# The second product of 512-row expert tiles, made as seven products of quarters behind the transforms

## The chip, the cores and the metric

The kernel runs on one core of one Trainium2 chip. The core has TensorE (PE; its weight loads are shown apart as PEld), VectorE (DVE), ScalarE (ACT), GpSimd (POOL) and SyncE (SP), which issue their instructions in order, each from its own queue. The metric is the time of one execution on the device in microseconds.

## The reference

The first block filters eight sequences of 2496 tokens with 256 features in the frequency domain; the second sends each of the 19968 filtered tokens through one of eight experts, the one with the largest logit.

```python
X = np.fft.rfft(x, axis=1)                       # x: (8, 2496, 256)
y = np.fft.irfft(X * (filt_r + 1j * filt_i), n=2496, axis=1)
x = y.reshape(19968, 256)
logits = x @ w_gate                              # 8 experts
e = argmax(logits); gate = softmax(logits)[e]
h = np.maximum(x @ w1[e], 0.0)                   # 256 -> 1024, for the rows of expert e
out = gate * (h @ w2[e])                         # 1024 -> 256
```

All operands are 32-bit floats. The two expert products are the bulk of the work.

## The kernel before, in words

**Transforms and routing.** The Fourier transforms are made as small matrix products in four stages (`stage_a` to `stage_d`), batch after batch. Behind each batch its tokens are routed: the logits are made, each token gets a row in a list of its expert, and POOL scatters the rows to a DRAM tensor, `rows`. After each batch a tile map (`tile_map`, line 839) takes full tiles out of the lists, so that expert tiles run beside the transforms of later batches.

**Expert tiles.** A tile is 512, 256 or 128 rows of one expert. `TILES` lists their sizes: 28 tiles of 512 rows in all, then 256-row tiles of the last batch (`PLACE` is the first of these) and 128-row tiles (`SHORT` is the first). For each tile SP loads the rows (`xg`, `ng`), DVE transposes them to `xT` (`turn_x`), and two streams of work on TensorE follow, in an order found while the program is built:

- The first product (`first_products`, `hidden_by_quarters`) makes h = relu(x·w1), one half of its 1024 columns after the other, into two buffers `hT` of a tile. For 512-row tiles, and for the 256-row tiles of the last batch, each half is made by seven products of quarters instead of eight: POOL first makes sums of quarters of x (`sums`, four operations) and of w1 (`wsum`, four operations per half, `w1_sums`), and DVE adds the products up. A half has 14 matmuls.
- The second product (`second_products`, `result`) makes 128 rows of the output at a time: eight matmuls of 128x128 weights (a piece of h) with 256 columns of w2, accumulated in one PSUM bank. DVE or ACT multiplies by the gate into `ys` (four buffers), and POOL scatters `ys` to the output with an indirect DMA. Each scatter to the output waits on the semaphore of the one before it, since both write the same tensor.

**Weights.** SP loads the two halves of a tile's w1 (`w1t`, three buffers) and w2 (`w2t`, two buffers) with `weights`, which `prefetch` calls when a buffer is free. Once the transforms are done (`late` is set), w2 of all experts is loaded piece by piece to stay (`w2s`), for the tiles from `PLACE` on, and the padding at the ends of the eight lists is scattered to `rows` by POOL (`pad_rows`, eight scatters), one with each call of `result` in the last batch.

**Order.** `Order` estimates when each engine is free and each tile is ready, and the loop at the end of the kernel picks the next transform step or expert product by these times. The order of instructions in each queue is fixed in this way when the program is built; on the chip, semaphores alone decide when each starts. The seven PSUM banks of the pool `ps` are given out in turn. All recorded operations show line 238, the one that issues them.

The lines that the steps below touch:

```python
w2t[h] = pools["moe"].tile([P, FH2, D], F32, tag="w2t", name="w2t", bufs=2)        # weights
h - used[what] < ((3 if h < 2 * SHORT else 8) if what == "w1" else 2 if h < 2 * PLACE else 8)   # prefetch
yield lambda: result(i, j), 3.42, ("w2", 2 * i + 1)                               # second_products
moe_w2=inputs["moe_w2"].reshape(E, 2, FT // 2, P, D).transpose(0, 1, 3, 2, 4),     # host
```

Of the kernel before, what the change touches and what calls it, by code (L numbers as in the profile page):

```python
# [19 lines left out]
P = 128  # L20
S = 2496
D = 256
E = 8
# [15 lines left out]
FT = F // P  # L39
# [227 lines left out]
def kernel(  # L267
# [55 lines left out]
    one = perm.tile([1, E], F32, name="one")  # L323
# [3 lines left out]
    ps = open_pool(ctx, name="ps", bufs=7, space=PSUM)  # L327
# [26 lines left out]
    vld = cst.tile([P, 2 * NG + 2], F32, name="vld")  # L354


    first = ExitStack()
    pro = open_pool(first, name="pro", bufs=2, side="right")
    tau_i = pro.tile([1, 32], I32, name="tau_i", bufs=1)
    e_i = pro.tile([P, E], I32, name="e_i", bufs=1)  # L360
    pools = {}
# [5 lines left out]
    def bank():  # L367
        return ps.tile([P, 512], F32, tag="bank", name="bank")


    t = nc.t
# [527 lines left out]
    FH2 = FT // 2  # L899
    TILES = [(rows // P, b) for b, g in enumerate(GROUPS) for rows, n in g for _ in range(n)]  # L900
    NT = len(TILES)
# [2 lines left out]
    SHORT = next(i for i in range(NT) if TILES[i][0] == 1)  # L904

    PLACE = next(i for i in range(NT) if TILES[i] == (2, B - 1))
    late = {}

    def quarters(i):
# [23 lines left out]
    def weights(h, second):  # L933

        i, k = divmod(h, 2)
        if late and second:

            for _ in range(1 if i < PLACE else 2 * E):
                if late["n"] < 2 * E:
                    e, hf = divmod(late["n"], 2)  # L940
                    nc.sync.dma_start(out=late["w2s"][:, e, hf * FH2:(hf + 1) * FH2], in_=moe_w2[e, hf])
                    late["n"] += 1
        if second and i >= PLACE:
            return
        ev = nc.sync.value_load(work[i][1], min_val=0, max_val=E - 1)
        if second:
            w2t[h] = pools["moe"].tile([P, FH2, D], F32, tag="w2t", name="w2t", bufs=2)
            nc.sync.dma_start(out=w2t[h], in_=moe_w2[bass.ds(ev, 1), k].rearrange("o p i d -> p (o i) d"))
        else:
            pool, bufs = (late["w1"], 8) if i >= SHORT else (pools["moe"], 3)  # L950
            w1t[h] = pool.tile([P, DH, 2, 2 * P], F32, tag="w1t", name="w1t", bufs=bufs)
            nc.sync.dma_start(out=w1t[h], in_=moe_w1[bass.ds(ev, 1), k].rearrange("o p i h f -> p (o i) h f"))
# [16 lines left out]
    def w1_sums(h):  # L969

        w = w1t[h]
        ts = wsum[h] = pools["moe"].tile([P, 3, 2 * P], F32, tag="wsum", name="wsum", bufs=2)
        nc.gpsimd.tensor_tensor(ts[:, 0], w[:, 0, 1], w[:, 1, 1], op=ALU.add)
        nc.gpsimd.tensor_tensor(ts[:, 1], ts[:, 0], w[:, 0, 0], op=ALU.subtract)

        nc.gpsimd.tensor_tensor(w[:, 0, 1], w[:, 0, 0], w[:, 0, 1], op=ALU.subtract)
        nc.gpsimd.tensor_tensor(ts[:, 2], w[:, 1, 0], ts[:, 1], op=ALU.subtract)
# [64 lines left out]
    def result(i, j):  # L1042
        n, e, r, b = work[i]
        if i >= PLACE:
            ev = nc.tensor.value_load(e, min_val=0, max_val=E - 1)
        if b == B - 1 and i < SHORT:
            next(late["pads"], None)
        p = bank()
        for k in range(FT):
            w2 = late["w2s"][:, bass.ds(ev, 1), k, :] if i >= PLACE else w2t[2 * i + k // FH2][:, k % FH2, :]  # L1050
            mm(p[:, :D], lhsT=hs[i][k % 4 // 2][:, k // 4, k % 2, j * P:(j + 1) * P], rhs=w2, start=(k == 0), stop=(k == FT - 1))
        ys = pools["moe"].tile([P, D], F32, tag="ys", name="ys", bufs=4)
        gate = gis[i][:, j, 8:9]
        either(p, D, lambda: nc.vector.tensor_scalar(ys, in0=p[:, :D], scalar1=gate, scalar2=None, op0=ALU.mult),
               lambda: nc.scalar.activation(ys, p[:, :D], AF.Copy, scale=gate))
        nc.gpsimd.indirect_dma_start(
            out=out,
            out_offset=bass.IndirectOffsetOnAxis(ap=gis[i].bitcast(U32)[:, j, :1], axis=0),
            in_=ys,
            in_offset=None,  # L1060
            bounds_check=N - 1,
            oob_is_err=False,
        )


    sides = []

# [62 lines left out]
    for k in range(B + 1):  # L1130
        steps = slot(k)
# [54 lines left out]
    def prefetch():  # L1186

        i = got["x"]
        if i < min(len(work), NT - RARE) and rows_at[work[i][3]] <= t["tensor"] and i - used["x"] < 2:
            rows_in(i)  # L1190
            asked.add(("x", i))
            got["x"] += 1
        for what in ("w1", "w2"):
            h = got[what]
            if h < 2 * min(len(work), NT - RARE) and rows_at[work[h // 2][3]] <= t["tensor"] and (
                    h - used[what] < ((3 if h < 2 * SHORT else 8) if what == "w1" else 2 if h < 2 * PLACE else 8)):
                weights(h, what == "w2")
                asked.add((what, h))
                got[what] += 1
        for h in range(used["w1"], got["w1"]):  # L1200
            if quarters(h // 2) and h not in wsum and len(wsum) < 2 and nc.ready(w1t[h]) <= max(t["tensor"], t["gpsimd"]) + 0.3:
                w1_sums(h)

    def when(key):

        what, n = key
        i = n // 2
        if what == "w2":
            if halves[0] <= n or key not in asked:
                return None  # L1210
            return max(ps.free("bank"), nc.ready(*hs[i], *((late["w2s"],) if i >= PLACE else (w2t[2 * i], w2t[2 * i + 1]))))
        if key not in asked or what != "x" and n % 2 and ends[0] < i:
            return None
        if what == "x":
            return nc.ready(xgs[n]) if t["vector"] < nc.ready(xgs[n]) else 0.0
        if what == "w1":
            return max(ps.free("bank"), nc.ready(w1t[n], xts[i]))
        return max(ps.free("bank"), ps.free("bank", 1) - 0.85, nc.ready(wsum[n], sums[i], xts[i]))
# [40 lines left out]
    def second_products():  # L1259

        for i in range(NT - RARE):
            for j in range(TILES[i][0]):
                yield lambda: result(i, j), 3.42, ("w2", 2 * i + 1)
            hs.pop(i), gis.pop(i), w2t.pop(2 * i, None), w2t.pop(2 * i + 1, None)
            used["w2"] += 2
            ends[0] += 1

    def rare_tiles():

# [17 lines left out]
    with tc.manual_schedule(engines=None):  # L1287
# [35 lines left out]
        while fs or any(heads):  # L1323
            choice = [(f, wait_of(f)) for f in open_steps()]
            products = []
            for k in (turn, 1 - turn):
                ready_at = when(heads[k][2]) if heads[k] else None
                if ready_at is not None:
                    products.append((k, max(0.0, ready_at - t["tensor"])))
            known = bool(products)  # L1330
            choice[0 if credit > 0.0 or not fs else 1:0] = products
            choice = [c for c in choice if c[1] is not None]
            pick, late_by = next((c for c in choice if c[1] <= 0.2), min(choice, key=lambda c: c[1]) if choice else (None, 0.5))
            if late_by > 0.2:
                t["tensor"] += min(late_by, 0.5)
            elif isinstance(pick, int):
                heads[pick][0]()
                credit -= heads[pick][1]
                if heads[pick][1] > 0.0:
                    turn = 1 - pick  # L1340
                heads[pick] = next(streams[pick], None)
            else:
                fs.remove(pick)
                pick[1]()
                credit = (credit if known else 0.0) + share() * pick[3]
                left_t[0] -= pick[3]
            flush()
            more_loads()
            for _ in range(4):
                side()  # L1350
            if not fs and not sides and not late:
                fft.close()
                tail = late["tail"] = open_pool(ctx, name="tail", bufs=1)
                late["w1"] = open_pool(ctx, name="w1b", bufs=8)
                late["n"] = 0
                late["pads"] = pad_rows()
                late["w2s"] = tail.tile([P, E, FT, D], F32, name="w2s")
            prefetch()
            if used["x"] > SHORT and "need" not in late:
                late["need"] = nc.values_load(need, min_val=0, max_val=GROUPS[-1][-1][1])  # L1360
# [32 lines left out]
```

## Time and profile before

| What | Value |
|---|---|
| time before, median of 3 runs | 1496.27 us (1493.14 to 1499.45) |
| the profiled execution's own time | 1494.36 us |
| its span, first to last instruction | 1492.7 us |
| TensorE busy | 1451.7 us (97%) |
| DVE, ACT, POOL busy | 770.7, 471.8, 733.4 us |
| granted TensorE clock | 0.991 |
| second product from `w2t` | 1984 records of 256 columns (992 matmuls) |
| DVE hT<-bank,hT of 512 elements | 392, mean 686 ns |
| POOL scatters to the output | 161, mean 998 ns |

All times of single instructions come from the one profiled execution, whose own time stands 1.9 us below the median. The 1.7 us between its span and its time lie around the program. In the profile a busy share of TensorE near 100% says that its queue never runs dry; a group's "idle before" names what ended the waiting of that engine, and only where TensorE is the one that waits does it lengthen the run by itself. In timelines the columns are start in us, length in us, engine, line, operation, output<-inputs, shapes and count, and in brackets the idle time before it with what ended it.

### The profile page before, as it was taken

How to read it: one execution, taken by the hardware profiler on the slowest of the kernel's cores; microseconds unless marked ns; L12 is line 12 of the kernel's file. 1: busy time of each engine (PE TensorE's matmuls, PEld its weight loads, DVE VectorE, ACT ScalarE, POOL GpSimd, SP SyncE). 2: the span in 40 equal slices, each digit the busy share in tenths (PEclk: the TensorE clock that was granted, in tenths of full speed). 3: DMA queues.
4: the chain of work that ended last, by engine and by line, in shares of the span. 5: the costliest groups of instructions: out<-in, count | busy, mean ns of one | idle time of the engine just before them, and what ended most of it. 6: DMA issues, size and time to landing. Idle time of an engine off the chain costs nothing. (4 is left out here: it accounts for less than half of the span.)

```text
span 1492.7 us, 24448 instructions
## 1 busy us (share of the span) xinstructions
PE 1451.7 (97%) x7396; PEld 1148.8 (77%) x7396; DVE 770.7 (52%) x1732; ACT 471.8 (32%) x983; POOL 733.4 (49%) x1053
## 2 busy tenths in 40 slices
PE   8898997999989999999999999999999999999998
PEld 6553555776667777777787888887888889999997
DVE  4667677354577656565764555537344334441110
ACT  4453442333322233222233222222222222223332
POOL 3434455344446656554555756764546455741111
PEclk9999999999999999999999999999999999999999
DMA  9749889678767756474456545545455543456661
GB/s 255 252 152 333 289 306 295 207 258 280 251 182 229 219 157 169 131 239 128 128 152 196 130 117 149 147 139 145 151 178 176 167 146 106 117 187 179 181 179 52
DMA packets 216376, 278.10 MB, mean 186 GB/s; under 512 B 124131, under 2 KB 163708, under 8 KB 216245
## 3 DMA queue, kind: packets, MB, share of 16 engines
q1 hardware_dynamic: 197125, 233.19, 52.7%
q0 software_dynamic: 19120, 43.33, 8.3%
q8 instruction: 62, 1.02, 0.3%
q14 instruction: 69, 0.57, 0.1%
HBM read 196.45 MB, written 80.64 MB: 186 GB/s over the span
## 5 line engine op out<-in xcount | busy, mean ns | idle before, releaser
L238 DVE TENSOR_TENSOR hT<-bank,hT 128x512 f32<-128x512 f32 (+1 forms) x504 | 300.7, 627 | 298.9 <-PE bank L238 183.1
L238 PE MATMUL bank<-w2t,hT 128*128 128x256 f32 x1984 | 447.5, 382 | 1.0 <-DVE hT L238 0.5
L238 PEld LDWEIGHTS bank<-w2t,hT 128*128 128x128 f32 x1984 | 377.6, 191 | 62.9 <-issue 9.5
L238 POOL DMA_INDIRECT out_dram<-ys,ng x161 | 160.7, 998 | 459.7 <-ACT ys L238 183.3
L238 PE MATMUL bank<-xT,w1t 128*128 128x256 f32 (+1 forms) x1728 | 316.7, 329 | 0.3 <-DVE xT L238 0.3
L238 PEld LDWEIGHTS bank<-xT,w1t 128*128 128x128 f32 x1728 | 266.8, 192 | 36.5 <-issue 11.8
L238 ACT ACTIVATE hT<-hT 128x1024 f32<-128x1024 f32 (+1 forms) x144 | 133.9, 958 | 378.7 <-DVE hT L238 374.8
L238 POOL DMA_INDIRECT rows<-yo,row x176 | 180.3, 1025 | 69.0 <-POOL yo L238 36.0
L238 ACT ACTIVATE ys<-bank,ng 128x256 f32<-128x256 f32 x128 | 60.6, 473 | 369.6 <-PE bank L238 297.0
L238 PE MATMUL bank<-sums,wsum 128*128 128x256 f32 (+1 forms) x576 | 135.7, 358 | 2.8 <-DVE hT L238 1.8
L238 PE MATMUL bank<-w2s,hT 128*128 x592 | 132.6, 380 | 0.0
L238 PEld LDWEIGHTS bank<-w2s,hT 128*128 128x128 f32 x592 | 110.5, 191 | 13.6
L238 PEld LDWEIGHTS bank<-sums,wsum 128*128 128x128 f32 x576 | 101.2, 191 | 20.1 <-issue 7.3
L238 DVE TENSOR_TENSOR ys<-bank,ht 128x512 f32<-128x512 f32 x80 | 55.0, 688 | 81.9 <-PE bank L238 77.3
L238 PE MATMUL bank<-fin,tas 117*120 117x512 f32 x154 | 76.9, 620 | 11.9 <-DMA fin<-in_x_dram 11.9
L238 PE MATMUL bank<-fin,tds 120*128 120x512 f32 (+1 forms) x168 | 76.6, 576 | 6.0 <-DMA fin<-ud 6.0
L238 DVE STREAM_TRANSPOSE xT<-xg 128x512 f32<-128x512 f32 (+2 forms) x126 | 57.5, 494 | 44.2 <-PE bank L238 44.2
L238 PE MATMUL bank<-fin,tbs 128*128 128x512 f32 x140 | 72.6, 605 | 2.5 <-DMA fin<-zd 2.5
L238 ACT ACTIVATE hT<-bank 128x128 f32<-128x128 f32 (+1 forms) x192 | 58.1, 304 | 50.1 <-PE bank L238 42.4
L238 PE MATMUL bank<-ys,tcs 128*128 128x512 f32 x140 | 72.7, 604 | 1.0 <-DVE ys L238 1.0
L238 POOL TENSOR_TENSOR wsum<-w1t 128x256 f32<-128x256 f32 x72 | 53.4, 742 | 38.1 <-PE bank L238 36.5
L238 PE MATMUL bank<-xT,wsum 128*128 128x256 f32 (+1 forms) x288 | 68.3, 360 | 0.3 <-DVE hT L238 0.3
(150 smaller groups left out, 1491.5 us busy)
## 6 DMA issues: line engine op xcount, KB each, us to landing
w1t<-in_moe_w_dram SPq DMA_DIRECT2D x126, 512.0 KB
w2t<-in_moe_w_dram SPq DMA_DIRECT2D x68, 512.0 KB
fin<-in_x_dram SPq DMA_DIRECT2D x39, 512.0 KB
fin<-zd SPq DMA_DIRECT2D x35, 512.0 KB
ud<-uo SPq DMA_DIRECT2D x35, 512.0 KB
fin<-ud SPq DMA_DIRECT2D x35, 512.0 KB
zd<-zo SPq DMA_DIRECT2D x35, 480.0 KB
xg<-rows SPq DMA_DIRECT2D x112, 128.0 KB
```

The source lines that it names most:

```text
L238: return real(*args, **named)
```

## The change

For the 512-row tiles whose second product begins after the transforms (`late` is set, `i < LARGE`), the second product of a tile is one product of two matrices cut into quarters: 512 rows of h in two halves of 256, 1024 inner columns in two halves of 512 (the two `hT` buffers), 256 output columns in two halves of 128. Seven products of quarters take the place of eight. Each is 2 x 4 matmuls with 128 columns, in one bank: 56 matmuls of 128 columns per tile in place of 32 of 256.

- `h_sums`: DVE makes three combinations of quarters of h (1024 elements per partition each), two into new buffers `hsum` and one in place. A fourth is made in place within the third product.
- `w2_sums`: POOL makes four of w2 (512 elements each), three into `tsum` and one in place.
- `result_by_quarters`: the seven products, with seven additions on DVE from PSUM, one copy on ACT, and then all four scalings by the gate on ACT, two behind the sixth product and two behind the seventh. Each is followed by its scatter (`deliver`, the scatter taken out of `result`).
- Between the seven steps the building loop may put steps of the next tile's first product.
- w2 is laid on the host by halves of h, so that half 0 of w2 goes with `hT` buffer 0. `result` reads h in that order too.
- After the transforms two more `w2t` buffers lie in a pool `quads`, used in turn with the two old ones, so that w2 can be loaded two tiles ahead. `quads` is closed after the last of these tiles, and the eight `w1t` buffers of the 128-row tiles are opened then, in place of at the end of the transforms.
- The padding rows go with the calls of `result` that are left, those of the 256-row tiles.

```diff
+    LARGE = 1 + max(i for i in range(NT) if TILES[i][0] == 4)
...
-            w2t[h] = pools["moe"].tile([P, FH2, D], F32, tag="w2t", name="w2t", bufs=2)
+            w2t[h] = (late["quads"] if late and late["flip"] else pools["moe"]).tile([P, FH2, D], F32, tag="w2t", name="w2t", bufs=2)
+            if late and k:
+                late["flip"] = not late["flip"]
...
+    def h_sums(i):
+        a = [t.rearrange("p f v (r c) -> p r (f v) c", r=2) for t in hs[i]]
+        ss = hsum[i] = [late["quads"].tile([P, FH2, 2 * P], F32, tag="hsum", name="hsum", bufs=3) for _ in range(2)]
+        nc.vector.tensor_tensor(ss[0], a[0][:, 1], a[1][:, 1], op=ALU.add)
+        nc.vector.tensor_tensor(ss[1], ss[0], a[0][:, 0], op=ALU.subtract)
+        nc.vector.tensor_tensor(a[0][:, 1], a[0][:, 0], a[0][:, 1], op=ALU.subtract)
+
+    def w2_sums(i):
+        w = [w2t[2 * i + g].rearrange("p k (n d) -> p n k d", n=2) for g in range(2)]
+        ts = tsum[i] = late["quads"].tile([P, 3, FH2, P], F32, tag="tsum", name="tsum", bufs=2)
+        nc.gpsimd.tensor_tensor(ts[:, 0], w[0][:, 1], w[0][:, 0], op=ALU.subtract)
+        nc.gpsimd.tensor_tensor(ts[:, 1], w[1][:, 1], ts[:, 0], op=ALU.subtract)
+        nc.gpsimd.tensor_tensor(ts[:, 2], w[1][:, 0], ts[:, 1], op=ALU.subtract)
+        nc.gpsimd.tensor_tensor(w[0][:, 1], w[1][:, 1], w[0][:, 1], op=ALU.subtract)
+
+    def result_by_quarters(i):
...
+        def product(left, right):
+            q = bank()[:, :D].rearrange("p (j d) -> p j d", j=2)
+            for j in range(2):
+                for k in range(FH2):
+                    mm(q[:, j], lhsT=left[:, k, j * P:(j + 1) * P], rhs=right[:, k], start=k == 0, stop=k == FH2 - 1)
+            return q
...
+        def send(j, y):
+            ys = pools["moe"].tile([P, D], F32, tag="ys", name="ys", bufs=4)
+            nc.scalar.activation(ys, y.rearrange("p n d -> p (n d)"), AF.Copy, scale=gate[:, j])
+            deliver(i, j, ys)
...
+        q = product(a[0][:, 0], w[0][:, 0])
+        nc.scalar.copy(out=one, in_=q)
+        yield
+        q = product(a[1][:, 0], w[1][:, 0])
+        add(top[:, :, 0], q, one)
+        yield
+        q = product(ss[1], ts[:, 1])
+        add(two, q, one)
+        nc.vector.tensor_tensor(a[1][:, 0], a[1][:, 0], ss[1], op=ALU.subtract)
+        yield
+        q = product(a[0][:, 1], w[0][:, 1])
+        add(three, q, two)
+        yield
+        q = product(ss[0], ts[:, 0])
+        add(low[:, :, 1], q, three)
+        add(four, q, two)
+        yield
+        q = product(a[1][:, 1], ts[:, 2])
+        add(low[:, :, 0], q, three)
+        for j in range(2):
+            send(2 + j, low[:, j])
+        yield
+        q = product(a[1][:, 0], w[1][:, 1])
+        add(top[:, :, 1], q, four)
+        for j in range(2):
+            send(j, top[:, j])
+        yield
...
-                    h - used[what] < ((3 if h < 2 * SHORT else 8) if what == "w1" else 2 if h < 2 * PLACE else 8)):
+                    h - used[what] < ((3 if h < 2 * SHORT else 8) if what == "w1" else (4 if late and h < 2 * LARGE else 2) if h < 2 * PLACE else 8)
+                    and (what == "w2" or h < 2 * SHORT or ends[0] >= LARGE)):
...
-            for j in range(TILES[i][0]):
-                yield lambda: result(i, j), 3.42, ("w2", 2 * i + 1)
+            if late and i < LARGE:
+                for j in range(7):
+                    yield go, 1.79, ("wide", 2 * i + 1)
+            else:
+                for j in range(TILES[i][0]):
+                    yield lambda: result(i, j), 3.42, ("w2", 2 * i + 1)
...
-        moe_w2=inputs["moe_w2"].reshape(E, 2, FT // 2, P, D).transpose(0, 1, 3, 2, 4),
+        moe_w2=inputs["moe_w2"].reshape(E, 2, 2, 2, P, D).transpose(0, 2, 4, 1, 3, 5).reshape(E, 2, P, FT // 2, D),
```

More of the change, by code (lines that the diff above doesn't have):

```diff
@@ L354 @@
     vld = cst.tile([P, 2 * NG + 2], F32, name="vld")
-    first = ExitStack()
+    first, quads = ExitStack(), ExitStack()
     pro = open_pool(first, name="pro", bufs=2, side="right")
@@ L946, in weights @@
         if second:
-            w2t[h] = pools["moe"].tile([P, FH2, D], F32, tag="w2t", name="w2t", bufs=2)
+            w2t[h] = (late["quads"] if late and late["flip"] else pools["moe"]).tile([P, FH2, D], F32, tag="w2t", name="w2t", bufs=2)
+            if late and k:
+                late["flip"] = not late["flip"]
             nc.sync.dma_start(out=w2t[h], in_=moe_w2[bass.ds(ev, 1), k].rearrange("o p i d -> p (o i) d"))
         else:
+            if i >= SHORT and "w1" not in late:
+                late["w1"] = open_pool(ctx, name="w1b", bufs=8)
             pool, bufs = (late["w1"], 8) if i >= SHORT else (pools["moe"], 3)
@@ L1050, in result @@
             w2 = late["w2s"][:, bass.ds(ev, 1), k, :] if i >= PLACE else w2t[2 * i + k // FH2][:, k % FH2, :]
-            mm(p[:, :D], lhsT=hs[i][k % 4 // 2][:, k // 4, k % 2, j * P:(j + 1) * P], rhs=w2, start=(k == 0), stop=(k == FT - 1))
+            mm(p[:, :D], lhsT=hs[i][k // FH2][:, k % FH2 // 2, k % 2, j * P:(j + 1) * P], rhs=w2, start=(k == 0), stop=(k == FT - 1))
         ys = pools["moe"].tile([P, D], F32, tag="ys", name="ys", bufs=4)
@@ L1055, in result, with deliver @@
                lambda: nc.scalar.activation(ys, p[:, :D], AF.Copy, scale=gate))
+        deliver(i, j, ys)
+    def deliver(i, j, ys):
         nc.gpsimd.indirect_dma_start(
@@ L1063, in result @@
         )
+    hsum, tsum, needs = {}, {}, {}
+    def h_sums(i):
[4 more added lines that the diff above has]
+        nc.vector.tensor_tensor(a[0][:, 1], a[0][:, 0], a[0][:, 1], op=ALU.subtract)
@@ new lines, in result_by_quarters, with part, add @@
+    def result_by_quarters(i):
+        a = [t.rearrange("p f v (r c) -> p r (f v) c", r=2) for t in hs[i]]
+        w = [w2t[2 * i + g].rearrange("p k (n d) -> p n k d", n=2) for g in range(2)]
+        gate = gis[i][:, :, 8:9]
+        def product(left, right):
[4 more added lines that the diff above has]
+            return q
+        def part(name):
+            return late["quads"].tile([P, 2, P], F32, tag=name, name=name, bufs=1)
+        def add(o, q, b):
+            nc.vector.tensor_tensor(o, q, b, op=ALU.add)
+        def send(j, y):
+            ys = pools["moe"].tile([P, D], F32, tag="ys", name="ys", bufs=4)
+            nc.scalar.activation(ys, y.rearrange("p n d -> p (n d)"), AF.Copy, scale=gate[:, j])
+            deliver(i, j, ys)
+        one, two, three, four = (part(name) for name in ("one", "two", "three", "four"))
+        top, low = (late["quads"].tile([P, 2, 2, P], F32, tag=name, name=name, bufs=1) for name in ("top", "low"))
+        q = product(a[0][:, 0], w[0][:, 0])
+        nc.scalar.copy(out=one, in_=q)
+        needs[i] = [hs[i][1]]
+        yield
+        q = product(a[1][:, 0], w[1][:, 0])
+        add(top[:, :, 0], q, one)
+        needs[i] = None
+        yield
+        ss, ts = hsum[i], tsum[i]
+        q = product(ss[1], ts[:, 1])
+        add(two, q, one)
+        nc.vector.tensor_tensor(a[1][:, 0], a[1][:, 0], ss[1], op=ALU.subtract)
+        needs[i] = []
+        yield
[10 more added lines that the diff above has]
+            send(2 + j, low[:, j])
+        needs[i] = [hs[i][1]]
+        yield
[3 more added lines that the diff above has]
+            send(j, top[:, j])
+        hsum.pop(i), tsum.pop(i), needs.pop(i)
+        yield
@@ L1202, in prefetch @@
                 w1_sums(h)
+        i = used["w2"] // 2
+        if late and i < LARGE and halves[0] > 2 * i + 1 and i not in hsum and ends[0] == i and i in wide and nc.ready(*hs[i]) <= max(t["tensor"], t["vector"]) + 0.3:
+            h_sums(i)
+        for i in (used["w2"] // 2, used["w2"] // 2 + 1):
+            if late and i < LARGE and (i in wide or i > used["w2"] // 2) and i not in tsum and len(tsum) < 2 and 2 * i + 1 in w2t and nc.ready(w2t[2 * i], w2t[2 * i + 1]) <= max(t["tensor"], t["gpsimd"]) + 0.3:
+                w2_sums(i)
+    wide = set()
     def when(key):
@@ L1211, in when @@
             return max(ps.free("bank"), nc.ready(*hs[i], *((late["w2s"],) if i >= PLACE else (w2t[2 * i], w2t[2 * i + 1]))))
+        if what == "wide":
+            if halves[0] <= n or ("w2", n) not in asked:
+                return None
+            more = needs.get(i, [hs[i][0], w2t[2 * i]])
+            if more is None:
+                if i not in hsum or i not in tsum:
+                    return None
+                more = [*hsum[i], tsum[i]]
+            return max(ps.free("bank"), nc.ready(*more))
         if key not in asked or what != "x" and n % 2 and ends[0] < i:
@@ L1261, in second_products, with go @@
         for i in range(NT - RARE):
-            for j in range(TILES[i][0]):
-                yield lambda: result(i, j), 3.42, ("w2", 2 * i + 1)
+            if late and i < LARGE:
+                wide.add(i)
+                steps = None
+                for j in range(7):
+                    def go():
+                        nonlocal steps
+                        steps = steps or result_by_quarters(i)
+                        next(steps)
+                    yield go, 1.79, ("wide", 2 * i + 1)
+            else:
+                for j in range(TILES[i][0]):
+                    yield lambda: result(i, j), 3.42, ("w2", 2 * i + 1)
             hs.pop(i), gis.pop(i), w2t.pop(2 * i, None), w2t.pop(2 * i + 1, None)
@@ L1266, in second_products @@
             ends[0] += 1
+            if ends[0] == LARGE:
+                quads.close()
     def rare_tiles():
@@ L1353 @@
                 tail = late["tail"] = open_pool(ctx, name="tail", bufs=1)
-                late["w1"] = open_pool(ctx, name="w1b", bufs=8)
                 late["n"] = 0
@@ L1357 @@
                 late["w2s"] = tail.tile([P, E, FT, D], F32, name="w2s")
+                late["flip"] = True
+                late["quads"] = open_pool(quads, name="quads", bufs=1)
             prefetch()
```

## The prediction

> **What bounds the kernel now.** The summary by slices comes first: is one engine full throughout? Then the busy time by stage, for the stage that the change touches.
>
> ```profile
> PE   8898997999989999999999999999999999999998
> PEclk9999999999999999999999999999999999999999
> 1020.00:1237.00 217.00, 216.67 (x1019) 191.26 (x1018) 93.53 (x161) 53.53 (x75) 114.13 (x149) 1.00 0.53 164
> 1237.00:1330.00 93.00, 93.00 (x626) 87.31 (x625) 45.61 (x120) 24.46 (x51) 60.50 (x90) 1.00 0.50 150
> ```
>
> The third line is the stage after the transforms (start:end, length, busy PE, weight loads, DVE, ACT, POOL, clock, DMA share, GB/s): TensorE idles 0.3 us of 217, at the full clock, with DVE at 43% and POOL at 53%. So TensorE's time is the time, as long as nothing else takes over. The fourth line, the 256-row tiles that follow, is as full. TensorE's timeline gives the prices:
>
> ```profile
> 1187.80 1.89 PE L238 MATMUL bank<-xT,w1t 128*128 128x256 f32 x8
> 1213.70 1.89 PE L238 MATMUL bank<-xT,w1t 128*128 128x256 f32 x8
> ...
> 1263.00 1.05 PE L238 MATMUL bank<-xT,w1t 128*128 128x128 f32 x8
> 1263.89 0.61 PE L238 MATMUL bank<-sums,wsum 128*128 128x128 f32 x4
> ```
>
> A matmul leaves two records. From 1187.80 to 1213.70 runs one whole 512-row tile: 28 matmuls of the first product and 32 of the second, all of 256 columns, 25.90/60 = 0.4317 us each. With 128 columns, 8 records (4 matmuls) take 0.89 us: 0.223 us each. The weight load of 191 ns, overlapping itself, does not hold them up.
>
> The next two views are of what the change loads more. POOL's timeline where it has results to scatter:
>
> ```profile
> 1153.46 0.99 POOL L238 DMA_INDIRECT out_dram<-ys,ng  x1 [0.30 <-issue]
> 1154.76 0.98 POOL L238 DMA_INDIRECT rows<-fill,pad  x1 [0.30 <-issue]
> 1156.69 0.99 POOL L238 DMA_INDIRECT out_dram<-ys,ng  x1 [0.96 <-DMA out_dram<-ys,ng]
> 1157.98 0.98 POOL L238 DMA_INDIRECT rows<-fill,pad  x1 [0.31 <-issue]
> 1159.88 0.99 POOL L238 DMA_INDIRECT out_dram<-ys,ng  x1 [0.92 <-DMA out_dram<-ys,ng]
> ```
>
> A scatter into the output waits until the one before it has landed: two never start closer than 3.2 us, while a scatter into another tensor fits between. And DVE beside POOL, where both operands of DVE's addition are in SBUF:
>
> ```profile
> 584.00 0.73 POOL L238 TENSOR_TENSOR xT<-xT 128x256 f32<-128x256 f32 x1
> 584.31 0.96 DVE L238 TENSOR_TENSOR ys<-ys,yw 128x512 f32<-128x512 f32 x1
> 584.68 1.18 POOL L238 TENSOR_TENSOR sums<-xT,sums 128x256 f32<-128x256 f32 x1
> ```
>
> DVE's takes 0.69 alone (median 693 ns), here 0.96; POOL's next 1.18 instead of 0.73. They exclude one another, and POOL loses 0.45 us to a DVE operation of 512 elements.
>
> **What the Trainium skill says.** "SBUF — State Buffer", Who interferes with whom: a DVE instruction with two SBUF inputs contends with a GpSimd instruction that reads SBUF; one waits for the other whole. The three lines above agree. "DMA: Bandwidth & Descriptors", Anatomy of one DMA: about 2.0 us fixed for a DMA from POOL's queue, mostly the write's receipt. With 0.98 of issue that makes about 3 us, and the trace has 3.2. "TensorE: Matmul & The Clock Gate", Back-to-back issue gap: N/2.4 + 2.5 ns; four such gaps are 223 ns for 128 columns and 437 for 256, and the trace has 223 and 432 (the factor 4 is the trace's, not the page's).
>
> **The change, part by part.** In the built program exactly eight 512-row tiles lie behind the transforms; the order up to there is the same on TensorE, and the new layout of w2 moves the same bytes.
>
> 1. TensorE. Removed per tile: 32 × 0.4317 = 13.81. Added: 56 × 0.223 = 12.49. Gain 1.32, by eight: **−10.6 us**. A tile's period goes from 25.90 to 24.58.
>
> 2. DVE. Added per tile: four SBUF-only operations of 1024 elements (three in h_sums, one in the third product) and seven of 256 from PSUM at 0.42; removed: one scaling of 0.48. No row has the 1024: from 64 elements (0.27) to 512 (0.69) is 0.95 ns an element, so about 1.18. With fourteen additions and two transposes at 0.686 that is 11.0 + 4.7 + 2.9 = 18.6 of 24.58, and with a wait of up to 0.73 for POOL at each SBUF-only one 21.5. It fits; its cover is TensorE's own work. The queue: h_sums stand before the additions of the next tile's first half, so seven PSUM banks must outlast them. In the steady order (product 1, four products of the next tile, product 2, ...) the additions are due again only when the bank ring comes round, some 7 us later: 0. In the first of the eight tiles a whole half (6 us, seven banks) goes before product 1, and product 2 then waits for a bank: 0 to 2.6, I take **+1**.
>
> 3. POOL. Added: four subtractions of 512 elements at 1.27 (the row ys<-ys,yw on POOL). Moved: the four scatters of a tile, 3.45 us apart before with w1 sums between, now stand in a row behind the last product. They take 3 × 3.2 + 1.0 = 10.6 us in which POOL, in order, does nothing else. Per tile: twelve w1 and x sums at 0.73 = 8.7, w2 sums 5.1, scatters 10.6: 24.4 of 24.58. So POOL is full, before any conflict with DVE. Each conflict with a 1024-element DVE operation costs it about 1 us (0.45 × 1.18/0.69 = 0.8, or up to 1.2 for the whole operation). Between 0 and 4 of them fall on POOL's arithmetic rather than into its waits; following one period, h_sums fall at the scatters' end in the first tile and into their waits later, and the fourth falls on sums: 1 to 2 per tile. POOL falls back 1 to 2 us a tile: by the seventh tile's scatters 6 to 12, and I take 9. Who waits for it: inside the stage nearly nobody, as the w1 sums behind a tile's scatters are used 10 us or more later. But in the 256-row tiles the period is 28 × 0.223 + 16 × 0.4325 = 13.2, and the w1 sums behind the eighth tile's scatters are due 14.4 us after these are ready (the rest of its last product 0.4, two halves of 3.1, two results 6.9, two products 0.9); scatters and two sums need 12. With some 3.6 us that POOL would wait before these scatters, lateness beyond about 6 reaches TensorE. POOL can't catch up there at first: eight sums of 0.73, four of 0.456, a pad, two output scatters: 5.8 + 1.8 + 1.3 + 4.2 = 13.1 of 13.2. The pads are new there: all eight stood beside 512-row tiles before, and two go with each of the first four 256-row tiles now, one of them between the output scatters. Two or three of these tiles lose 0.5 to 1 each, 2 in all, even without lateness (0 where POOL runs ahead). So 9 − 6 + 2 = **+5**; its ends are 0 and 26, as the second rival has them.
>
> 4. SP and ACT. The same loads, w2 up to two tiles ahead instead of one: at first 2 MB ahead of a w1 half that is needed over 30 us later, 0. w1 of the one-block tiles waits for the end of the 512-row tiles, 90 us before its use, 0. ACT gains two of the four scalings (it has 25% busy), 0. The pads must land before the one-block tiles' rows are read, 30 us or more later: 0.
>
> Sum: −10.6 + 1 + 5 = −4.6. The profiled execution was 1494.36 (span 1492.7 and 1.7 around it), so 1489.8 for its like. The median of the runs shown is 1496.27, 1.9 above it: **1491.7**. Half a per cent, 7.5 us, is about what a measurement can tell from no change.
>
> **The rivals.**
>
> *POOL keeps up.* Conflicts fall into its waits, less than 1 us a tile is lost, the lateness stays under 6, and the bank wait is short: −10.6 + 0 to 2.5, so 1485.7 to 1488. For it: POOL waits 10 us in each row of scatters, and that is where h_sums would fall once it is a little late. Against it: 24.4 of 24.58 leaves no room at all.
>
> *POOL becomes the bound, and the kernel slower.* The place: POOL's queue from the row of scatters to the next. If it loses d a tile, the change is −10.6 + 1 + (6d − 6) + 2 = 6d − 13.6. It decides from d = 2.3, and passes half a per cent at 3.5. The ends of d: −0.2, and four conflicts of 1.2 with some scatters held up too (one beside a DVE addition took 1421 ns instead of 992): 5, so +16, 1513. For it: every part of this is in the trace. Against it: lateness itself moves the scatters' waits under h_sums.
>
> *DVE becomes the bound.* It would need 3 us more than the 21.5, in waits for POOL's 1.27 us operations; each full wait adds 0.5, four make 2. At most some 0.5 us a tile: −10.6 + 4 + 5 + 1, about 1496.
>
> *The change does not do what it says.* If narrow matmuls ran at their weight load's 0.19 per record, 56 × 0.38 = 21.3 us would lose 60; the lines at 1263 exclude it.
>
> **How the numbers follow.** Partly eaten gain 0.50 (with the DVE case, all within half a per cent: 1489 to 1503), POOL keeping up 0.33 (faster), POOL as the bound 0.17 (slower; 1504 to 1513). The range leaves out the far end of the last: 1484.5 to 1506. The likeliest alone: 1489 to 1499.
>
> **What would show it.** TensorE: quarter matmuls at 0.223, a tile's period at 24.6, and idle time at wsum in the first 256-row tiles, ended by POOL. POOL: output scatters in fours 3.2 us apart, their row starting later from tile to tile by 1 to 2 us; its sums at 1.1 to 1.9 where h_sums run. It is wrong if the periods are not 24.6, if scatters stand closer than 3.2, if POOL's rows don't slip, or if TensorE waits for DVE in each tile.

## The result: slower by 2.35 per cent, and the profile after

The changed kernel takes **1532.1 us** (median of 6 runs, 1527.4 to 1536.2), the kernel before 1497.8 beside it; the ratio is 1.0235, with an interval of [1.0213, 1.0256]. The profiled execution has a span of 1528.3 us against 1492.7. TensorE's own timeline splits the 35.6 us. The stretches are cut at the start of the first tile by quarters (in the kernel before, of the same tile) and at the starts of second products in the 256-row tiles; the last ends with TensorE's last matmul, 6.1 us before the span's end in both traces:

| stretch | before | after | difference |
|---|---|---|---|
| up to the first 512-row tile by quarters | 1032.40 | 1034.64 | +2.2 |
| the eight tiles, up to the first 256-row tile's results | 210.53 | 231.34 | +20.8 |
| to the second 256-row tile's results | 13.16 | 22.06 | +8.9 |
| the next three 256-row tiles | 39.48 | 43.03 | +3.5 |
| the rest | 190.99 | 191.10 | +0.1 |

The first row is no effect of the change: in the traces of the experiments below, whose code is the same up to there, this point lies anywhere between 1029.9 and 1040.9. The change costs 33.3 us behind it.

First the window of the eight tiles before the change (start:end, length, busy PE, weight loads, DVE, ACT, POOL, granted clock, DMA share, GB/s):

```profile
1032.40:1242.93 210.53, 210.53 (x1017) 186.84 (x1016) 88.52 (x149) 53.52 (x77) 113.22 (x150) 1.00 0.53 163
```

And windows of some tiles after it; each of the first five begins where a tile's first half does, the last is the second 256-row tile:

```profile
1060.95:1085.55 24.60, 24.60 (x171) 23.15 (x170) 17.65 (x27) 7.26 (x11) 13.32 (x16) 1.00 0.61 173
1085.55:1114.58 29.03, 26.64 (x171) 24.00 (x169) 18.88 (x27) 7.25 (x11) 20.47 (x21) 0.94 0.51 146
1114.58:1141.45 26.87, 25.13 (x171) 22.98 (x170) 18.68 (x27) 7.27 (x11) 16.85 (x16) 1.00 0.53 154
1141.45:1175.23 33.78, 27.66 (x170) 24.86 (x169) 19.69 (x27) 7.27 (x11) 22.98 (x24) 0.90 0.37 122
1175.23:1203.65 28.42, 25.14 (x171) 22.99 (x170) 19.24 (x27) 7.25 (x11) 20.57 (x21) 1.00 0.46 139
1265.98:1288.04 22.06, 16.20 (x90) 15.18 (x89) 7.78 (x22) 3.41 (x7) 11.64 (x18) 0.85 0.29 82
```

One undisturbed period is 24.60, to the hundredth what the prediction's first step gives (24.58). From the next on the periods are 26.3 to 33.8, TensorE idles in them, and in some the granted clock falls to 0.94, 0.90 and 0.85. The waits of TensorE from 1034 to 1332 (total, times, longest) name one engine:

```profile
PE bank L238 <- POOL wsum L238: 25.5, 12, 5.9
PE bank L238 <- POOL w1t L238: 2.0, 4, 0.5
PE bank L238 <- DVE hT L238: 1.5, 1, 1.5
```

And one turn of POOL, out of the timeline of all engines (start, duration, engine, operation, in brackets idle time and what ended it):

```profile
1122.98 0.73 POOL L238 TENSOR_TENSOR wsum<-w1t 128x256 f32<-128x256 f32 x1
...
1123.65 1.23 DVE L238 TENSOR_TENSOR hsum<-hT 128x1024 f32<-128x1024 f32 x1 [0.27 <-ACT hT L238]
...
1123.79 1.66 POOL L238 TENSOR_TENSOR wsum<-wsum,w1t 128x256 f32<-128x256 f32 x1
1124.91 1.63 DVE L238 TENSOR_TENSOR hsum<-hsum,hT 128x1024 f32<-128x1024 f32 x1
1125.42 1.70 POOL L238 TENSOR_TENSOR w1t<-w1t 128x256 f32<-128x256 f32 x1
...
1125.51 1.13 PE L238 MATMUL bank<-sums,wsum 128*128 128x256 f32 x4 [1.21 <-POOL wsum L238]
...
1126.46 1.74 DVE L238 TENSOR_TENSOR hT<-hT 128x1024 f32<-128x1024 f32 x1
1127.08 1.70 POOL L238 TENSOR_TENSOR wsum<-w1t,wsum 128x256 f32<-128x256 f32 x1
...
1128.94 0.99 POOL L238 DMA_INDIRECT out_dram<-ys,ng  x1 [0.16 <-issue]
...
1131.94 0.36 SPq L238 DMA_DIRECT2D w1t<-in_moe_w_dram  x1
1132.15 0.98 POOL L238 DMA_INDIRECT out_dram<-ys,ng  x1 [2.21 <-DMA out_dram<-ys,ng]
1132.34 0.43 SPq L238 DMA_DIRECT2D w2s<-in_moe_w_dram  x1
...
1138.91 0.98 POOL L238 DMA_INDIRECT out_dram<-ys,ng  x1 [5.78 <-DMA out_dram<-ys,ng]
...
1142.22 0.98 POOL L238 DMA_INDIRECT out_dram<-ys,ng  x1 [2.33 <-DMA out_dram<-ys,ng]
1143.22 0.74 POOL L238 TENSOR_TENSOR wsum<-w1t 128x256 f32<-128x256 f32 x1
...
1144.82 1.13 PE L238 MATMUL bank<-sums,wsum 128*128 128x256 f32 x4 [1.48 <-POOL wsum L238]
```

Three things are to be seen. The w1 sums beside the three h_sums take 1.66 to 1.70 instead of 0.73: 0.95 us lost, three times. (DVE's additions and POOL's sums exclude one another, as the prediction's lines show; this is called the lock below.) The four scatters stand in a row, and two neighbours are 3.2, then 6.8, then 3.3 us apart: the one that was issued between two loads of 512 KB (w1t and w2s) takes 5.78 us to land instead of 2.2. And the first sums behind the row are what TensorE waits for at 1144.82. More often it waits for the set after them: at 1125.51 it waits for w1 sums that stand behind the x sums and the w2 sums, at the end of POOL's turn. Of the 19.6 us that TensorE waited for POOL ahead of the first 256-row results, 18.1 are of this kind. Over seven such rows, from a row's first scatter to the sums behind it, POOL spends 14.9, 12.0, 14.3, 13.3, 11.3, 12.3 and 11.7 us: 12.8 in the mean.

That POOL is full, its groups from 1060 to 1230 show: the only idle time of any weight before its instructions is ended by a landing, and none of it by TensorE.

```profile
L238 POOL DMA_INDIRECT out_dram<-ys,ng x24 | 24.6, 1025 | 54.3 <-DMA out_dram<-ys,ng 53.4 <-issue 0.8
...
L238 POOL TENSOR_TENSOR w1t<-w1t 128x256 f32<-128x256 f32 x11 | 12.9, 1174 | 0.0
```

A tile's load on POOL is thus about 8.7 (w1 and x sums) + 5.1 (w2 sums) + 12.8 (row) + 2.9 (lost beside h_sums) = 29.5, with the loss of a tile whose three h_sums all meet w1 sums. Its sums behind the rows start at 1083.29 and, six rows later, at 1257.15: 28.98 us a tile. POOL sets the period, and it falls 4.4 us behind TensorE's 24.6 in each.

The costliest single wait lies where the stage ends, in the second 256-row tile:

```profile
1272.89 1.05 PE L238 MATMUL bank<-xT,w1t 128*128 128x128 f32 x8
1279.81 1.22 PE L238 MATMUL bank<-sums,wsum 128*128 128x128 f32 x4 [5.86 <-POOL wsum L238]
1280.82 1.06 PE L238 MATMUL bank<-xT,w1t 128*128 128x128 f32 x4
1281.67 1.06 PE L238 MATMUL bank<-sums,wsum 128*128 128x128 f32 x4
...
1285.81 0.61 PE L238 MATMUL bank<-sums,wsum 128*128 128x128 f32 x4
```

After 5.86 us of idling four records start 0.85 us after the four before them, and from 1285.81 on 0.45 again: matmuls at half speed for 6 us, some 3 us on top of the wait. Wait and slow matmuls make the 8.9 of the table.

### The profile page after: what moved, and what is told of

Same layout as the page of the kernel before. It is cut to its first block, busy times and chain, and to the rows that moved or that the text cites. A ratio compares the mean times of both kernels' runs of the same rounds, so it can differ in the third digit from the quotient of the medians.

```text
span 1528.3 us, 25422 instructions
## 1 busy us (share of the span) xinstructions
PE 1457.5 (95%) x7780; PEld 1157.9 (76%) x7780; DVE 837.3 (55%) x1812; ACT 477.8 (31%) x999; POOL 795.5 (52%) x1085
## 5 line engine op out<-in xcount | busy, mean ns | idle before, releaser
L238 PE MATMUL bank<-w2t,hT 128*128 128x256 f32 (+1 forms) x1984 | 398.6, 356 | 2.7 <-DVE hT L238 2.0
L238 PEld LDWEIGHTS bank<-w2t,hT 128*128 128x128 f32 x1984 | 342.8, 192 | 53.5 <-issue 9.3
L238 PE MATMUL bank<-xT,w1t 128*128 128x256 f32 (+1 forms) x1728 | 321.8, 332 | 3.7 <-POOL w1t L238 2.0
L238 PEld LDWEIGHTS bank<-xT,w1t 128*128 128x128 f32 x1728 | 267.9, 193 | 42.8 <-issue 12.4
L238 POOL DMA_INDIRECT rows<-yo,row x176 | 181.4, 1030 | 69.0 <-POOL yo L238 29.4
L238 PE MATMUL bank<-sums,wsum 128*128 128x256 f32 (+1 forms) x576 | 140.4, 368 | 28.1 <-POOL wsum L238 26.5
L238 ACT ACTIVATE ys<-bank,ng 128x256 f32<-128x256 f32 x104 | 49.3, 474 | 304.5 <-PE bank L238 233.7
L238 PE MATMUL bank<-sums,w1t 128*128 128x256 f32 (+1 forms) x288 | 68.1, 360 | 0.0
```

Of the source, the lines that this page charges most:

```text
L238: return real(*args, **named)
```

## The experiments

Theory A: POOL's queue is the bound; the row of scatters, each waiting for the landing of the one before, is the largest part of it, the w2 sums and the lock with h_sums are the rest. Theory B: the lock is what delays TensorE, and the scatters' waits are idle time that would be had anyway. More rivals come with the runs that test them. Ratios are to the kernel before, run beside it on the same chip; the changed kernel stands at 1.0235. Where an experiment leaves sums out, the output is no longer the product, and only the time is read.

**Free scatters.** The scatters write rows of their own, so their order can be given up, in all tiles:

```diff
-        nc.gpsimd.indirect_dma_start(
+        sc = nc.gpsimd.indirect_dma_start(
             out=out,
...
         )
+        tc.declare_no_dep(sc.ins, group="results", reason="rows of their own")
+        tc.add_to_no_dep_group("results", sc.ins)
```

> The changed kernel with one edit: the scatters into the output no longer wait for one another's landing. Theory A (POOL's queue is the bound, and the row of scatters its largest part): the trace gives POOL 8.7 of w1 and x sums, 5.1 of w2 sums, 12.8 for a row of four scatters and 2.9 lost to h_sums, 29.5 us a tile against TensorE's 24.6; without the waits a row is 4 x 1.3 = 5.2 and the load 21.9, so the waits at wsum (25.5 us) and the slow matmuls behind them (15 us) go: 1486 to 1495 us, periods of 24.6. Theory B (the lock between h_sums and the w1 sums is what delays TensorE, the scatters' waits being idle time that would be had anyway): little changes, 1515 to 1530, with the waits at wsum still above 15 us.

Measured: **1487.4 us, ratio 0.9931 [0.9906, 0.9957]**. The whole loss is gone and the change becomes a gain. POOL's timeline:

```profile
1136.92 0.99 POOL L238 DMA_INDIRECT out_dram<-ys,ng  x1 [0.37 <-ACT ys L238]
1138.22 0.98 POOL L238 DMA_INDIRECT out_dram<-ys,ng  x1 [0.30 <-issue]
1139.50 0.98 POOL L238 DMA_INDIRECT out_dram<-ys,ng  x1 [0.30 <-ACT hT L238]
1140.79 0.98 POOL L238 DMA_INDIRECT out_dram<-ys,ng  x1 [0.30 <-issue]
1143.51 0.72 POOL L238 TENSOR_TENSOR wsum<-w1t 128x256 f32<-128x256 f32 x1 [1.74 <-PE bank L238]
```

The scatters are 1.3 us apart, and then it is POOL that waits for TensorE. Here h_sums still draw POOL's sums out, in places more than in the changed kernel (three x sums at 1.7, a w2 sum at 2.26), and it costs nothing. So the row decides, and B falls.

> The kernel before with the same edit (the scatters into the output don't wait for one another). TensorE idles 0.3 us of 217 in the stage, so theories A and B both expect no change: 1494 to 1500. If it gains 3 us or more, the scatters' waits cost the kernel before too, and a gain of the first run is not the change's alone.

Measured with the same edit in the kernel before: 1497.2 us, ratio 1.0007 [0.9996, 1.0019]. The gain is not one that the kernel before could have had; there the scatters' landings are covered.

> The changed kernel with the output scatters free of one another, once more and in more rounds, as the version that may beat both: 1484 to 1491 us, 0.4 to 0.8 per cent below the kernel before. If its gain came from the chip of that call: within 0.3 per cent of it.

Measured again: **1488.9 us, ratio 0.9948 [0.9930, 0.9966]**. This version beats both kernels. Its window from the first tile by quarters to the first 256-row tile's results, to be held against 210.53 before:

```profile
1037.10:1237.68 200.58, 200.39 (x1401) 189.34 (x1400) 154.27 (x226) 58.85 (x93) 172.39 (x168) 1.00 0.52 160
```

**Without w2 sums.** In `w2_sums` the four subtractions are only counted in the planner, and three products read quarters of w2:

```diff
-        nc.gpsimd.tensor_tensor(ts[:, 0], w[0][:, 1], w[0][:, 0], op=ALU.subtract)
+        planned("gpsimd", ts[:, 0], w[0][:, 1], w[0][:, 0])
...
-        q = product(ss[1], ts[:, 1])
+        q = product(ss[1], w[1][:, 0])
```

> The changed kernel without its w2 sums: three of the seven products read a quarter of w2 in their place, so the second product's values are others; the instructions of the other engines keep their order. Theory A: 5.1 us of POOL go, 29.5 becomes 24.4 of 24.6; TensorE waits hardly at all: 1488 to 1502. Theory B: the lock stays (three h_sums a tile, about 1 us each), 1510 to 1525.

Measured: 1490.8 us, ratio 0.9968 [0.9955, 0.9981], as A has it. All periods are 24.6, though the row is still there, at 12.1 to 15.7 us. More than the 5.1 us went: in most turns one w1 sum is drawn out to 1.7 instead of three, since the other h_sums fall into the row. But the results of the first five 256-row tiles follow one another at 14.5, 14.1, 14.0 and 15.8 us instead of 13.16: 5.7 us are lost there even where POOL keeps up within the stage. The last scatter of the eighth tile ends 5.7 us after the first of these results began (1236.15 and 1230.49); in the kernel before it ended 4.3 us ahead of it (1238.66 and 1242.93).

**Without h_sums.** The three additions are only counted, and products read parts of h:

```diff
-        nc.vector.tensor_tensor(ss[0], a[0][:, 1], a[1][:, 1], op=ALU.add)
+        planned("vector", ss[0], a[0][:, 1], a[1][:, 1])
...
-        ss, ts = hsum[i], tsum[i]
+        ss, ts = [a[0][:, 1], a[1][:, 1]], tsum[i]
```

> The changed kernel without h_sums (three additions of 1024 elements a tile on DVE): three products read parts of h in their place, so the second product's values are others; the order of the other instructions is kept. Theory A: the lock's 2.9 us a tile go, POOL has 26.6 of 24.6, falls back 2 us a tile, and from the fifth tile TensorE waits again: 1498 to 1512, between the two kernels. Theory B: with the lock gone the waits at wsum go: 1486 to 1495.

Measured: 1514.4 us, ratio 1.0123 [1.0081, 1.0164], between the two kernels, 2 us above A's band and far above B's. A was right in kind, not in its size: TensorE waits from the third tile on, not from the fifth, as the first full row takes 16.9 us here. The same w1 sums as above, in the same stretch:

```profile
L238 POOL TENSOR_TENSOR w1t<-w1t 128x256 f32<-128x256 f32 x13 | 9.5, 727 | 0.0
```

727 ns instead of 1174: POOL's loss beside h_sums is gone, and with h_sums goes about half of the kernel's loss. (DVE's time for them goes too; "One input instead of two" below tries to tell the two apart.) Without them POOL still has more than 24.6 (26.2 a tile in the mean), and TensorE still waits 15.5 us for its sums. The terms don't add up to the loss one by one: it is gone as soon as POOL's turn is below 24.6, so 7.9 off the row (12.8 to 4.9, the scatters being free) or the w2 sums with two of the three conflicts take all of it, 2.9 off the lock do not.

**Loads doubled beside the row.**

```diff
                     nc.sync.dma_start(out=late["w2s"][:, e, hf * FH2:(hf + 1) * FH2], in_=moe_w2[e, hf])
+                    tc.nc.sync.dma_start(out=late["w2s"][:, e, hf * FH2:(hf + 1) * FH2], in_=moe_w2[e, hf])
```

> The changed kernel; each load of w2s (512 KB; two stand in a tile, each straight behind another load) is issued twice. In the changed kernel a scatter lands 2.2 us after its issue ends where no load was just issued, but 3.4 to 5.8 us after where two loads were. Theory A1 (the loads stretch the landings, and so the row of scatters, 12.8 instead of 10.6 us): 1 to 3 us more in each of seven rows, 1537 to 1553 us. Theory A2 (the long landings have another cause, such as the scatter's own rows): 1528 to 1536, as the changed kernel.

Measured: 1545.0 us, ratio 1.0310 [1.0264, 1.0357], clear of the changed kernel's interval. The profiled execution took 1557.7 us, 12 us more than any of the other three, so its lines are read for which scatter lands late, not for sizes:

```profile
1143.25 0.99 POOL L238 DMA_INDIRECT out_dram<-ys,ng  x1 [0.15 <-issue]
...
1146.25 0.36 SPq L238 DMA_DIRECT2D w1t<-in_moe_w_dram  x1
...
1146.44 0.98 POOL L238 DMA_INDIRECT out_dram<-ys,ng  x1 [2.20 <-DMA out_dram<-ys,ng]
1146.66 0.42 SPq L238 DMA_DIRECT2D w2s<-in_moe_w_dram  x1
...
1153.28 0.98 POOL L238 DMA_INDIRECT out_dram<-ys,ng  x1 [5.86 <-DMA out_dram<-ys,ng]
```

A scatter without a load just before it lands in 2.20, the next, between loads, in 5.86. TensorE waits for POOL's sums as before, and never for a load, so the doubled loads cost through POOL. A1 holds: loads that are under way stretch a scatter's landing. How much longer the rows became is not read from this one execution. The kernel before has such a landing too, with two loads straight behind the start of a scatter:

```profile
1134.32 0.99 POOL L238 DMA_INDIRECT out_dram<-ys,ng  x1 [0.94 <-DMA out_dram<-ys,ng]
1134.46 0.34 SPq L238 DMA_DIRECT2D w2t<-in_moe_w_dram  x1
1134.85 0.43 SPq L238 DMA_DIRECT2D w2s<-in_moe_w_dram  x1
...
1142.33 0.99 POOL L238 DMA_INDIRECT out_dram<-ys,ng  x1 [5.73 <-DMA out_dram<-ys,ng]
```

**Two tiles by quarters instead of eight.** `LARGE` is lowered by 6, and w2t's second pool is used below it only.

> Only the first two of the eight tiles by quarters, the other six as before. Theory A (POOL falls back 4.4 us a tile, and TensorE waits only once a slack of some 7 to 8 us is gone): two tiles bring 2 x -1.32 and +1, and at most 1 to 2 us of waits: 1493 to 1498 us. Theory C (each tile by quarters costs by itself, 36.6/8 = 4.6 us): 1503 to 1507.

Measured: 1496.7 us, ratio 1.0012 [0.9994, 1.0031]: A's 1493 to 1498, short of C's 1503. TensorE doesn't wait for POOL once, and the stage takes 209.91 us against 210.53. The cost is not in a tile by itself but in the lateness that tiles add up.

**The same scatters, spread.** `send` puts its scatters in a list, and one is taken from it behind every second w1 sum, behind the x sums and behind two w2 sums:

```diff
         nc.gpsimd.tensor_tensor(ts[:, 1], ts[:, 0], w[:, 0, 0], op=ALU.subtract)
+        post()
...
-            deliver(i, j, ys)
+            outbox.append((gis[i], j, ys))
```

> The changed kernel with the same scatters, still each waiting for the last one's landing, but put between POOL's sums: one behind every second w1 sum, behind the x sums and behind two w2 sums. Theory A says the row is what costs, not the number of scatters: the sums fill the landings, POOL has 8.7 + 5.1 + 4 + 2.9 and 3 to 5 of waits that remain, 24 to 26 us a tile: 1490 to 1505 us. If the wait for each landing costs POOL the same wherever the scatter stands: 1525 to 1537.

Measured: 1504.7 us, ratio 1.0069 [1.0040, 1.0097]: A's band, at its upper end. With each scatter still waiting for its predecessor's landing, but with sums to do meanwhile, most of the loss goes (0.0166 of 0.0235). What is left are waits that the new order makes: 6.7 us for wsum, 5.8 for ACT, 2.3 for h_sums.

**More work for TensorE.** Ahead of a half's third product, four matmuls into a bank that nothing reads:

```diff
+        if late and i < LARGE:
+            q = bank()[:, :n * P].rearrange("p (v c) -> p v c", v=2)
+            for _ in range(2):
+                for v in range(2):
+                    tc.nc.tensor.matmul(q[:, v], lhsT=w[:, 1, 0][:, v * P:(v + 1) * P], rhs=b[:, 1, 0], start=True, stop=True)
         q = product(ws[:, 1], ts[:, 1])
```

> The changed kernel with 64 more matmuls on TensorE, four in each half of a late 512-row tile ahead of its third product, into a bank that nothing reads: 64 x 0.43 = 27.6 us of TensorE's time, 3.45 a tile. Theory A (POOL is the bound in the whole stage, TensorE's idle time and its slow matmuls behind that idle time are only its reflection): TensorE's tile becomes 28.0 of POOL's 29.0, 1527 to 1538, no change within 5 us. Theory D (TensorE's slow matmuls are a cost of their own, 15 of the 44 us lost): filling the idle time keeps the clock up, 1515 to 1525. If TensorE is the bound: 1550 to 1562.

Measured: 1523.9 us, ratio 1.0194 [1.0159, 1.0229]. 27.6 us of added matmuls do not make the kernel slower; if anything it is some 6 us faster, just below A's band and inside D's. The waits of TensorE from 1030 to 1345:

```profile
PE bank L238 <- POOL wsum L238: 3.4, 5, 1.0
```

All of that is in the 256-row tiles; in the stage the periods are 28.04, TensorE's own 24.58 + 3.45. So TensorE had these 3.45 us to spare in the changed kernel, and POOL needs no more than 28.04 here where it needed 28.98. The timeline says why: between two rows POOL spends 14.8 to 15.0 us, in the first four turns of the changed kernel 16.8 to 16.9. With TensorE no longer waiting for POOL, h_sums fall into the row's waits and not on w1 sums, as the lines of one turn show:

```profile
1105.19 0.98 POOL L238 DMA_INDIRECT out_dram<-ys,ng  x1 [2.23 <-DMA out_dram<-ys,ng]
...
1107.15 1.23 DVE L238 TENSOR_TENSOR hsum<-hT 128x1024 f32<-128x1024 f32 x1 [0.26 <-ACT hT L238]
...
1108.41 1.23 DVE L238 TENSOR_TENSOR hsum<-hsum,hT 128x1024 f32<-128x1024 f32 x1
...
1109.17 1.31 POOL L238 DMA_INDIRECT out_dram<-ys,ng  x1 [3.01 <-DMA out_dram<-ys,ng]
```

D is not excluded as a part: the matmuls run at full speed here (a granted clock of 1.00 over the stage), and how much of the gain is theirs is not known. In the stage of the changed kernel slow matmuls can't have held POOL up directly, as it never waited for TensorE from 1060 to 1230.

**One input instead of two.**

```diff
+    def one_input(o, left, right):
+        nc.count("vector", "tensor_tensor", (o, left, right), {})
+        tc.nc.vector.tensor_scalar(o, in0=left, scalar1=0.5, scalar2=None, op0=ALU.mult)
...
-        nc.vector.tensor_tensor(ss[0], a[0][:, 1], a[1][:, 1], op=ALU.add)
+        one_input(ss[0], a[0][:, 1], a[1][:, 1])
```

(and likewise the other two, each counted in the planner as an addition)

> The changed kernel with each of the three h_sums as a multiplication of the same 1024 elements by a constant: one input in SBUF instead of two, at the same place of DVE's order and for the same readers (the values of the second product are others). If it is the lock of two SBUF inputs that draws POOL's w1 sums out to 1.7 us, they run at 0.73 as without h_sums: 1508 to 1520 us. If DVE's time or the waits on its results cost, the lock being a side effect: 1526 to 1537.

Measured: 1523.7 us, ratio 1.0192 [1.0164, 1.0220], between the two bands. The timeline shows that the question was put too simply:

```profile
1123.92 0.74 POOL L238 TENSOR_TENSOR wsum<-w1t 128x256 f32<-128x256 f32 x1
1124.42 0.78 DVE L1078 TENSOR_SCALAR hsum<-hT 128x1024 f32<-128x1024 f32 x1
1124.73 1.05 POOL L238 TENSOR_TENSOR wsum<-wsum,w1t 128x256 f32<-128x256 f32 x1
1125.24 1.10 DVE L1078 TENSOR_SCALAR hsum<-hsum 128x1024 f32<-128x1024 f32 x1
1125.75 1.17 POOL L238 TENSOR_TENSOR w1t<-w1t 128x256 f32<-128x256 f32 x1
```

The operation with one input takes less time on DVE, but it excludes POOL's sums as well: 1.05 to 1.17 us, not 0.73. The Trainium skill ("SBUF — State Buffer", Who interferes with whom) says that a tensor_scalar can run in a mode that takes the shared ports; this trace agrees. The time falls with what POOL loses (three times 0.4 instead of 0.95), which speaks for the lock as the way in which h_sums cost. But DVE's own time for them falls too, and an operation of DVE's of the same length that doesn't touch POOL was not tried: this stays argued.

**The pads.** In the kernel without w2 sums, `send` issues one pad ahead of each result of the first two tiles:

```diff
+            next(late["pads"], None)
             ys = pools["moe"].tile([P, D], F32, tag="ys", name="ys", bufs=4)
```

> The kernel without w2 sums (1490.8 us), with the eight pads put back beside 512-row tiles, one ahead of each result of the first two. There the four 256-row tiles from the second 256-row result on lose 5.7 us (periods 14.5, 14.1, 14.0, 15.8 instead of 13.16). If the pads between the scatters make this loss: periods of 13.2 and 1483 to 1488 us. If the four landings themselves or POOL's lateness make it: 1489 to 1494.

Measured: 1489.4 us, ratio 0.9959 [0.9944, 0.9973], the same as with the pads in the 256-row tiles. The results follow at 14.79, 13.38, 16.65 and 13.16: 5.3 us are lost without a single pad there, where POOL waits up to 7.0 us ahead of the second scatter of a tile. So the pads don't make this loss. That the ordered landings do is likely: with free scatters and the pads in the 256-row tiles (the first experiment) the results follow at 13.2 to 13.3 us. But there POOL was not late either, and the trace doesn't name what ended the wait of 7.0.

## Why the prediction was wrong

It said 1491.7 us, 1484.5 to 1506, and gave "slower" 17 chances in 100; it came out at 1532. Its second rival named the right mechanism (POOL's queue from one row of scatters to the next), but ended it at 1513.

- **Step 1, TensorE: right.** −10.6 us and a period of 24.58; the undisturbed period is 24.60. (The gap that the prediction takes from the skill's page is that of an isolated matmul; for a stream with weight loads the page itself gives a longer one. The price came from the trace, and it held.) Where POOL is out of the way (free scatters) the stage takes 200.58 instead of 210.53: −9.95, against −10.6 + 1 predicted.
- **Step 2, DVE: right.** The one wait of the first tile is 1.5 us (0 to 2.6, +1 taken); DVE is busy 17.3 to 20.2 us in a tile's period.
- **Step 4, SP and ACT: right where TensorE is concerned.** No wait of TensorE in the stage is for a load. But the loads act on POOL, which the step doesn't have.
- **Step 3, POOL: here it failed**, in four terms.
  1. The row of scatters, "3 × 3.2 + 1.0 = 10.6", is 12.8. 3.2 us is the distance with nothing else under way, the smallest that the trace of before has; loads of w1 and w2s beside the row stretch it to 6.8. Doubling the loads showed it. The trace of before had the case shown at that experiment, and it was passed over for the minimum.
  2. The conflicts, "1 to 2 per tile", are three in five of the eight tiles, 2.8 to 2.9 us in each.
  3. "Lateness itself moves the scatters' waits under h_sums" did not come about. In six of the eight tiles h_sums landed on w1 sums, in one on w2 sums, and in one in the row. They are due about when TensorE comes to the sums of a second half: in the turn shown they start at 1123.65, and TensorE is there at 1124.30. As TensorE waits for just these sums, POOL is making them at that time. With TensorE slowed down by added matmuls it did not wait, and h_sums fell into the row. That TensorE's waiting holds the two together is read from the timeline, not tested by itself.
  4. "Inside the stage nearly nobody" waits for POOL, since the sums behind a tile's scatters are used "10 us or more later": the w1 sums behind the first tile's row were there 2 us before TensorE took them (1084.85 and 1087.28), and at 1097.66 TensorE waited for the first time. What it mostly waited for, the second half's sums at the end of POOL's turn, the step doesn't have. Together: the 24.4 of the prediction plus 2.2 and 2.9 is 29.5, where 29.0 was measured.
- **The rival's formula**, 6d − 13.6, gives +13 with d = 4.4, and the measured change is +33. It sized the lateness as if a slack of 6 stood ahead of the 256-row tiles, where POOL came in with none, and for what the tiles behind pay it had 2 us: they paid 12.4, of which the kernel without w2 sums loses 5.7 even without lateness from tile to tile, and about 3 are matmuls at half speed after a wait.
- **The pads, 2 us in all,** were right about the place and wrong about the cause; see the last experiment.

What was said to prove it wrong, "if the periods are not 24.6", did so. What stays open is how much of the half speed of TensorE is a cost of its own: it is seen after the 5.86 us wait, outside of the stage that POOL bounds, but no run took it away by itself. Open too is how much of h_sums' cost is the lock and how much DVE's time.

## What to carry to other kernels

When work moves onto an engine that is in order, add up that engine's turn with its waits, not its busy time: here POOL's busy share in a full period was under 80 per cent, and it was the bound. A load that comes to 99 per cent of the period with the scatters at their smallest distance leaves nothing for anything else; take the terms' means under the traffic of that place, and ask what the new wait fixes in phase with what. And where writes go to rows of their own, say so: four ordered scatters cost 12.8 us of the queue, four free ones 4.9, and that alone turned a loss of 2.35 per cent into a gain of 0.5 to 0.7.

## What the runs showed of the hardware

- In the changed kernel's rows a scatter into DRAM lands 2.2 to 2.3 us after its issue has ended when SP had issued no load in the 1.5 us before it and none of 512 KB beside it, and 2.8 to 5.8 us after it otherwise. The Trainium skill ("DMA: Bandwidth & Descriptors", Anatomy of one DMA) gives a fixed cost of about 2.0 us; that is the floor here, not the value beside loads.
- A multiplication of 1024 elements by a constant on DVE, with one input in SBUF, drew POOL's 0.73 us sums out to 1.05 to 1.17; an addition with two inputs drew them out to 1.7.
- TensorE's matmuls ran at half speed (a granted clock of 0.54 from 1097.66 to 1101.20, 0.51 from 1279.80 to 1285.80) for some 3 to 6 us after waits of 2.4, 4.6, 4.2 and 5.9 us, and at full speed after others of 1.5 and 2.75. The Trainium skill ("TensorE: Matmul & The Clock Gate", Part 1) puts the return to half clock at an idle window of about 3.4 us that runs freely; one of the waits here is shorter than that and was followed by half speed all the same.
